# Seven graph hops and an attention block on one core: overflow sums held open at hop seams, bucket-pass work moved between ScalarE and VectorE, and a buffer of its own for hop 2's first matrices

## The chip, the core and the metric

One core of a Trainium2 chip runs the whole program. It has five engines that each take their instructions in order: PE (TensorE, matmuls), ACT (ScalarE), DVE (VectorE), POOL (GpSimd) and SP (SyncE, which here issues DMAs). The metric is the device time of one execution in microseconds (us), lower is better. Times of the profile are microseconds from the start of one profiled execution; "L844" is line 844 of the kernel before.

## The reference

A graph of 10,000 nodes and 160,000 directed edges, 128 features for each node. Seven times the features are propagated along the edges with a symmetric normalization. Each node then has eight tokens (its own features and the seven hops), which go through one self-attention block, and a readout weighs the eight results.

```python
h = x
toks = [x]
for _ in range(7):
    msg = h[src] * deg_inv_sqrt[src, None] * deg_inv_sqrt[dst, None]
    h = _segment_sum(msg, dst, N)
    toks.append(h)
tok = jnp.stack(toks, axis=1)                      # (N, K+1, D)
t = _layernorm(tok, axis=-1)
...
o = tok + jnp.einsum('nkd,de->nke', o, wo)
alpha = _softmax(jnp.einsum('nkd,d->nk', _layernorm(o, axis=-1), w_r), axis=-1)
return jnp.einsum('nk,nkd->nd', alpha, o)
```

## The kernel before, in words

**Layout.** The nodes are cut into 79 tiles of 128. The current features of all nodes lie in SBUF in a table `tab` (each value as a high and a low half of 16 bits, so a row has 256 columns), in two copies, one read and one written in a hop. A hop is done as matmuls with one-hot matrices: for one destination tile, 72 gather matmuls (L844) pick the source rows of its edges out of the table into PSUM tiles `p`, nine evictions (ACT L849 for five of them, DVE L851 for four) bring them to SBUF tiles `eb`, and 18 scatter matmuls (L819) add them into the destination's sum `acc` in PSUM. This is a *block*; a hop is 79 blocks, tiles 72 to 78 first and then 0 to 71. The blocks of a hop are numbered 0 to 78 in that order.

**Overflow rows.** An edge that doesn't fit into the fixed buckets of its tile is brought from a copy of the table in DRAM by an indirect DMA on POOL, `fetch` (L781). There are two of these for each tile: `og0` reads `tabh`, which holds the rows of the tiles from 72 on, and `og1` reads `tabd`, all rows; each is added with one more matmul (L804). The rows of the last tile of a hop reach `tabd` only after the hop's last block, so the `og1` of blocks 0 and 1 of the next hop (named `ogl`) come late: those two blocks add them at the close of the sum (L833), after their scatters. Closing a block also means a DVE reduction `s` (L835) and `entries` (L880 to L882: ACT, DVE, DVE), which make the next table's rows, and a scaling `r` on POOL (L889) and a store by SP. Scatters lag two evictions behind the gathers (`pend`), and the close of a block is done in the next one; between two hops stands a scaling step (a maximum over nodes, on PE, DVE and PE again: `pm`, `pb`).

**How hops are ordered.** Hops 2 to 7 are written block by block in Python and placed by the framework's scheduler; POOL, like the others, runs its queue in order. `ahead` asks the fetches of the block two further on; at the start of a hop it asks those of blocks 0 to 2 together.

**The second bucket pass and hop 1.** Before, a first pass over the edges has put them into buckets by source. The second pass places each bucket's edges by destination and makes the one-hot matrices `w` of each tile (written to DRAM as `gsd`, read again by the hops 2 to 7), and hop 1 runs beside it. It goes over 20 *quads* of four tiles (the first of three) in a software pipeline written by hand: the string FRONT is a list of words, each with a lag in sweeps, a letter for a step, and indices; `tc.manual_schedule` keeps this order on each engine. Sweep i does each word for quad i minus its lag. Steps that matter here: `O` (L493, one-hot of keys on DVE, L263), `X` (L517, a product `ux` on DVE for which `R` on PE waits, L524), `U` (L513, ACT), `a` (SP loads `rb` and `ra` from DRAM; one buffer for `rb`), `b` (L668, one DVE operation, 1408 columns of `w` from `rb`), `w` (L672, two ACT operations of 448 columns from `ra`), `G` (gather, L711), `x` (eviction, ACT L719 or DVE L721), `S` (scatter, L696 and L697) and `z` (DVE copies the in-degree, L735).

The eviction of the second pass picks its engine thus (before):

```python
if n < len(quads) - 1 or jj % 2 == 0:
    A.activation(e[:, :, 0:256], pv, AF.Copy, scale=8.0)
else:
    V.tensor_tensor(e[:, :, 0:256], pv, self.eight[:, :, None].to_broadcast([128, 2, 256]), op=ALU.mult)
```

The first matrices that hop 2 reads are loaded into a pool that is opened when the pools of hop 1 have been given back (L981). The attention's constants (L1100 to L1123) are made during hop 2; two of them start from iotas on POOL (L1106, L1116).

Of the kernel before, what the change touches and what calls it, by code (L numbers as in the profile page):

```python
# [7 lines left out]
F32 = mybir.dt.float32  # L8
# [16 lines left out]
CELL = 334  # L25
ROWS = 56
# [41 lines left out]
class Hops:  # L68
# [580 lines left out]
    def matrices(self, quads, Q):  # L649
# [17 lines left out]
        def b(q, g, t):  # L667
            V.tensor_scalar(q["w", g][:, NJ * 128:NJ * 128 + cut], q["rb", g], self.pid8, 0.125, op0=ALU.is_equal, op1=ALU.mult, saturate=False)  # L668
# [21 lines left out]
    def hop1(self, quads, Q):  # L690
# [23 lines left out]
        def x(q, g, t, n, jj):  # L714
            e = q["eb", g, jj] = ebuf[self.eb_i % len(ebuf)]
            self.eb_i += 1
            pv = q["p", g, jj].rearrange("p j h d -> p j (h d)")
            if n < len(quads) - 1 or jj % 2 == 0:
                A.activation(e[:, :, 0:256], pv, AF.Copy, scale=8.0)  # L719
            else:  # L720
                V.tensor_tensor(e[:, :, 0:256], pv, self.eight[:, :, None].to_broadcast([128, 2, 256]), op=ALU.mult)  # L721
# [50 lines left out]
    def fetch(self, t, i, src, name=None, after=None):  # L772
# [4 lines left out]
        else:  # L777
            o = self.ogp.tile([128, 256], F16, name=name or f"og{i}", bufs=2 if name else None)
# [6 lines left out]
    def block(self, t, w, tab, og, pend, lag, runs, first, evac, fin, lead=False, late=False, mid=None, ahead=None,  # L785
              after=None):


# [4 lines left out]
        def both(W, rows, start, stop=False):  # L793

            T.matmul(acc[0][:, :129], W, rows[:, 128:257], start=start, stop=False, skip_group_check=True)
            T.matmul(acc[0][:, :128], W, rows[:, :128], start=False, stop=stop, skip_group_check=True)


        def fetched(i, start=False, stop=False):
            W = w[:, (NG + i) * 128:(NG + i + 1) * 128] if i < NI else self.Sov[:, t, :]  # L800
            if first:
                both(W, og[i], False, stop)
                return
            T.matmul(acc[0][:, :256], W, og[i], start=start, stop=stop)  # L804

        def begin():
            acc.append(self.pacc.tile([128, 512], F32, name="acc", tag="acc"))
            for i in range(NI if late else NI + 1):
                fetched(i, start=i == 0)

        def scat(e, jj):
            if not acc:
                acc.append(self.pacc.tile([128, 512], F32, name="acc", tag="acc"))
            for j in range(e.shape[1]):
                J = 2 * jj + j
                if first:
                    both(w[:, J * 128:(J + 1) * 128], e[:, j], J == 0)
                else:
                    T.matmul(acc[0][:, :256], w[:, J * 128:(J + 1) * 128], e[:, j, :256], start=False, stop=J == NG - 1 and not late)  # L819
                if first and J == 0 and not lead:  # L820
                    for i in range(NI):
                        fetched(i)

        def close():
            if first:
                if lead:
                    for i in range(NI):
                        fetched(i)
                fetched(NI, stop=True)
                fin(t, acc[0][:, :128], acc[0])  # L830
                return
            if late:
                T.matmul(acc[0][:, :256], self.Sov[:, t, :], og[NI], start=False, stop=True)  # L833
            s = self.fp.tile([128, 128], F32, name="s")
            V.tensor_reduce(s, acc[0][:, 0:256].rearrange("p (h d) -> p d h", h=2), axis=X, op=ALU.add)  # L835
            fin(t, s, acc[0])
# [17 lines left out]
        jj = 0  # L854
        for i, n in enumerate(runs):
            for _ in range(n):
                gather(jj)
                if jj == 0 and not first and not mid:
                    ahead(self.ebuf[(self.eb_i - 1) % len(self.ebuf)][:, 0, 0:1])
                jj += 1  # L860
            if mid:
                mid(0)
            if not first:
                begin()
                if mid:
                    ahead()
            while len(pend) > lag:
                pend.pop(0)()
            if mid:
                mid(1)  # L870
            if after:
                after()
            if i == len(runs) - 1:
                pend.append(close)
            yield
# [17 lines left out]
    def run(self, ctx, att, nhop=K):  # L893
        tc, nc, V, A, T, G = self.tc, self.nc, self.nc.vector, self.nc.scalar, self.nc.tensor, self.nc.gpsimd
        with ExitStack() as c:
# [5 lines left out]
            G.memset(self.wB[:, 0], 0.0)  # L901
            base, self.ebuf = self.ebuf, []
            self.more_ebufs(self.bp, 8 - len(base))
            self.extra, self.ebuf = self.ebuf, base
            self.og1 = [[self.bp.tile([128, 260], F16, name=f"og{j}{b}") for b in range(2)] for j in range(NI + 1)]
            for o in (o for z in self.og1 for o in z):
                G.memset(o, 1.0)
            self.pass_a()
# [6 lines left out]
            Q = [dict() for _ in quads]  # L915
            words = [(int(z[0]), z[1], [int(k) for k in z[2:].split(".")]) for z in FRONT.split()]
            with tc.manual_schedule():
                do = {**self.place(quads, Q), **self.matrices(quads, Q), **self.hop1(quads, Q)}
                for i in range(len(quads) + max(z[0] for z in words)):
                    for late, z, more in words:  # L920
                        if 0 <= i - late < len(quads):
                            do[z](i - late, *more)
        with ExitStack() as c:
# [11 lines left out]
            pend = []  # L935
            for k in range(2, nhop + 1):
                i = 1 - k % 2
                tab, din = self.tab[i], (self.tabd[i], self.tabh[i])
# [20 lines left out]
                def fin(t, s, acc, k=k, ct=ct, last=last, i=i):  # L959
# [6 lines left out]
                order = [*range(4 * NG, NT), *range(4 * NG)]  # L966
# [605 lines left out]
```

## Time and profile before

| what | value |
|---|---|
| three timed executions, us | 3792.43, 3800.98, 3807.27 (median 3800.98) |
| the profiled execution's own time, us | 3793.14 |
| its span in the profile, us | 3791.4 |
| mean granted TensorE clock | 0.975 of full speed |
| first bucket pass | 0 to 345 us |
| second bucket pass and hop 1 | 345 to 1014.7 us |
| hops 2 to 7 | 1014.7 to about 3140 us |
| attention and readout | about 3146 us to the end |

How to read what follows. A row of a *timeline* has the start, the time from there to the end of the group, the engine, the line, the operation, output and input with their shapes, the number of instructions taken together, and in brackets the idle time just ahead of it with what ended it. "issue" is idle time in which the engine waited for nothing that the profile shows. A row of *waits* has the engine, the waiting tile and line, an arrow to what it waited for, then total us, number of times and longest. A row of *windows* has the stretch, its length, the busy time of PE, PE's weight loads, DVE, ACT and POOL with their instructions, the granted clock, the share of DMA and GB/s. A row of *groups* has line, engine, operation and shapes, the count, then busy us, mean ns of one, and idle time ahead with its releasers.

### The profile page before, as it was taken

The numbers are of one execution on the slowest core, as the hardware profiler recorded it, in microseconds if no ns is written. First come the engines' busy times: TensorE is split into PE (matmuls) and PEld (weight loads), VectorE is DVE, ScalarE is ACT, GpSimd is POOL, SyncE is SP. The second block draws the span as 40 slices with busy tenths as digits, with TensorE's granted clock in tenths as the row PEclk, the third lists the DMA queues.
The fourth block names the chain that finished last, engine by engine and source line by source line (L and its number), as shares of the span: only waits on it lengthen the run. The fifth ranks groups of instructions, "written<-read, shape, count | busy, mean of one in ns | idle before, by whom it ended". The sixth has DMA issues, their size and how long they took to land.

```text
span 3791.4 us, 174085 instructions
## 1 busy us (share of the span) xinstructions
PE 3563.0 (94%) x73922; PEld 2942.3 (78%) x73922; DVE 3030.7 (80%) x7077; ACT 2790.2 (74%) x7083; POOL 1687.0 (44%) x2231
## 2 busy tenths in 40 slices
PE   6777899999899999999999999999999998999997
PEld 4676677788688888887888788888878886777775
DVE  9999888899677777777777777777766665888888
ACT  7996688888766766766766676666656658888885
POOL 1000334444366656665666566566656661211111
PEclk8988899999999999999999999999999999999998
DMA  2011556566666666666666666666666552222220
GB/s 83 1 30 39 155 184 187 188 191 190 203 199 199 202 196 200 203 199 190 203 201 204 186 203 198 196 203 200 202 190 198 188 182 73 77 80 79 82 84 15
DMA packets 332729, 595.57 MB, mean 157 GB/s; under 512 B 57447, under 2 KB 225605, under 8 KB 326693
## 3 DMA queue, kind: packets, MB, share of 16 engines
q1 hardware_dynamic: 293989, 506.70, 42.9%
q0 software_dynamic: 35392, 72.55, 6.7%
q8 instruction: 579, 9.49, 1.0%
q10 hardware_dynamic: 2560, 5.12, 0.5%
q14 instruction: 209, 1.71, 0.2%
HBM read 455.49 MB, written 128.67 MB: 154 GB/s over the span
## 4 chain that ended last, share of the span: by engine, by line
PE 68%; DMA 2%; DVE 1%; issue 1%; ACT 1%; SPq 0%; ACTq 0%; DVEq 0%; POOLq 0%
PE p L844 26%; PE acc L819 24%; PE acc L804 4%; PE pv L1216 4%; PE pu L1200 4%; PE po L1235 2%; PE pt L1190 2%; PE ps L1265 1%; PE pf L1424 1%; PE sm L1271 1%; DMA og<-tabd,oidx 1%; DMA ogl<-tabd,oidx 0%; PE pf L1250 0%; DMA tabd<-tab 0%; ACT junk L1257 0%
## 5 line engine op out<-in xcount | busy, mean ns | idle before, releaser
L849 ACT ACTIVATE eb<-p 128x512 f16<-128x512 f32 x2370 | 1259.2, 601 | 506.7 <-PE p L844 296.3
L851 DVE TENSOR_TENSOR eb<-p,eight 128x512 f16<-128x512 f32 x1896 | 1220.3, 685 | 307.1 <-PE acc L819 187.0
L844 PE MATMUL p<-tab,w 128*32 128x256 f16 x34128 | 1036.0, 274 | 17.9 <-issue 12.3
L819 PE MATMUL acc<-eb,w 128*128 128x256 f16 x8532 | 1012.9, 273 | 2.3 <-DVE id L1119 1.6
L844 PEld LDWEIGHTS <-w 128*32 128x32 fp8e4 x34128 | 872.7, 97 | 155.2 <-issue 136.0
L819 PEld LDWEIGHTS <-w 128*128 128x128 fp8e4 x8532 | 835.8, 98 | 101.3 <-issue 3.2
L781 POOL DMA_INDIRECT og<-tabh,oidx x553 | 594.9, 1076 | 683.2 <-DVE eq L678 359.2
L781 POOL DMA_INDIRECT og<-tabd,oidx x541 | 577.4, 1067 | 559.0 <-PE acc L819 262.4
L719 ACT ACTIVATE eb<-p 128x512 f16<-128x512 f32 x695 | 373.8, 618 | 17.0 <-PE p L711 13.0
L889 POOL TENSOR_SCALAR r<-s,ctok 128x128 f32<-128x128 f32 x474 | 294.8, 622 | 47.3 <-DVE s L835 30.1
L880 ACT ACTIVATE tab<-s,c 128x128 f16<-128x128 f32 x395 | 158.5, 401 | 200.3 <-DVE eb L851 168.1
L881 DVE SCALAR_TENSOR_TENSOR tab<-s,c,tab 128x128 f16<-128x128 f32 x395 | 138.9, 352 | 180.6 <-issue 170.2
L1305 POOL TENSOR_TENSOR p<-e,in 128x1024 f32<-128x1024 f32 (+1 forms) x40 | 76.6, 1914 | 449.6 <-DVE e L1304 435.5
L1257 ACT ACTIVATE junk<-tab 128x128 f32<-128x128 f32 x626 | 248.4, 401 | 8.2 <-SPq L1541 6.8
L389 ACT ACTIVATE rs<-iof,rb 128x128 fp8e4<-128x128 f32 x832 | 251.6, 391 | 0.8
L711 PE MATMUL p<-tab,w 128*32 128x256 f16 x5688 | 205.7, 277 | 22.4 <-ACT eb L719 14.3
L835 DVE TENSOR_REDUCE s<-acc 128x128 f32<-128x256 f32 x474 | 196.4, 414 | 22.5 <-PE acc L833 14.5
L696 PE MATMUL acc<-eb,w 128*128 128x129 f16 x1422 | 204.2, 223 | 1.2 <-issue 0.8
L697 PE MATMUL acc<-eb,w 128*128 128x128 f16 x1422 | 202.3, 221 | 0.6 <-issue 0.6
L780 POOL COPY og<-eb 128x1 f16<-128x1 f16 x452 | 84.1, 186 | 252.2 <-ACT eb L849 252.1
L711 PEld LDWEIGHTS <-w 128*32 128x32 fp8e4 x5688 | 137.0, 96 | 58.2 <-issue 37.2
L1216 PEld LDWEIGHTS pv<-Wv,xT 128*64 128x64 f32 x2504 | 138.9, 137 | 44.8 <-ACT uT L1201 29.2
(322 smaller groups left out, 5233.9 us busy)
## 6 DMA issues: line engine op xcount, KB each, us to landing
w<-gsd SPq DMA_DIRECT2D x474, 592.0 KB
gsd<-w SPq DMA_DIRECT2D x79, 592.0 KB
tok<-r SPq DMA_DIRECT2D x546, 64.0 KB
tab<-tok SPq DMA_DIRECT2D x273, 128.0 KB
rb<-srow SPq DMA_DIRECT2D x79, 352.0 KB
tabd<-tab SPq DMA_DIRECT2D x396, 64.0 KB
ra<-srow SPq DMA_DIRECT2D x79, 224.0 KB
og<-tabh,oidx POOLq DMA_INDIRECT x553
```

The source lines that it names most:

```text
L389: A.activation(c["ro"][k][:, j - cuts[k][0], i, :], self.iof, AF.Abs_reciprocal_sqrt, scale=2.0 ** 21, bias=c["rb"][:, j - VP, i:i + 1], s ...
L696: T.matmul(acc[:, :129], W, rows[:, 128:257], start=start, stop=False, skip_group_check=True)
L711: T.matmul(p[32 * w:32 * w + 32, j], q["w", g][:, NJ * 128 + s * CAP:NJ * 128 + (s + 1) * CAP], tab[:, s, :], start=True, stop=True)
L719: A.activation(e[:, :, 0:256], pv, AF.Copy, scale=8.0)
L781: self.nc.gpsimd.indirect_dma_start(out=o[:, :256], out_offset=None, in_=src[0] if i == NI else src[1], in_offset=bass.IndirectOffsetOnAxi ...
L819: T.matmul(acc[0][:, :256], w[:, J * 128:(J + 1) * 128], e[:, j, :256], start=False, stop=J == NG - 1 and not late)
L844: T.matmul(p[32 * q:32 * q + 32, j], w[:, NJ * 128 + s * CAP:NJ * 128 + (s + 1) * CAP], tab[:, s, :], start=True, stop=True)
L849: A.activation(e[:, :n, 0:256], pv, AF.Copy, scale=8.0)
L851: V.tensor_tensor(e[:, :n, 0:256], pv, self.eight[:, :, None].to_broadcast([128, n, 256]), op=ALU.mult)
L889: self.nc.gpsimd.tensor_scalar(r, s, ct[:, t:t + 1], None, op0=ALU.mult)
L1216: T.matmul(p[64 * h:64 * h + 64, u - us[0], :], S[i]["xT"][:, h * m + q, 64 * c:64 * c + 64], Wv, start=True, stop=True, tile_position=(0, ...
L1257: A.activation(j, S[i]["x"][:, g, :], AF.Square, bias=S[i]["x"][:, g, 0:1], scale=-1.0, accum_out=R[i % 6][:, 0, g:g + 1])
```

## The change

It has seven parts.

1. `HEAD = 2`: for the first two quads (seven tiles) step `b` is done by two ACT operations of 704 columns instead of one DVE operation of 1408.
2. Evictions with odd number go to DVE in the last three quads instead of the last one.
3. The two first steps `O` are issued ahead of the first sweep.
4. The pool of the extra eviction tiles and of hop 1's overflow rows is opened after the first bucket pass.
5. Hop 2's first matrices have a buffer of their own, `wx`, loaded in the last sweep.
6. At the seams of hops the overflow sums are held open longer. Blocks 0 and 1 close after the scatters of blocks 2 and 3; blocks 2 and 3 sum into the other half of the PSUM tiles of blocks 0 and 1. Blocks 0 to 4 all add `og1` at their close. A table, LEAD, says in which block and behind which eviction each fetch of the first blocks is asked, and the first four `og0` of the next hop are asked in blocks 77 and 78. `og0` has six buffers instead of three.
7. The attention's two iotas are made when its object is made, at the program's start.

```diff
+HEAD = 2
...
         def b(q, g, t):
+            if q["n"] < HEAD:
+                new(q, g)
+                for a in range(0, cut, cut // 2):
+                    A.activation(q["w", g][:, NJ * 128 + a:NJ * 128 + a + cut // 2], q["rb", g][:, a:a + cut // 2], AF.Abs_reciprocal_sqrt,
+                                 scale=2.0 ** 14, bias=self.off, saturate=False)
+                return
             V.tensor_scalar(q["w", g][:, NJ * 128:NJ * 128 + cut], q["rb", g], self.pid8, 0.125, op0=ALU.is_equal, op1=ALU.mult, saturate=False)
...
-            if n < len(quads) - 1 or jj % 2 == 0:
+            if n < len(quads) - 3 or jj % 2 == 0:
...
+                early = [("O", 0, 0), ("O", 0, 1)]
+                for z, *a in early:
+                    do[z](*a)
+                sweeps = len(quads) + max(z[0] for z in words)
+                for i in range(sweeps):
+                    if i == sweeps - 1:
+                        nc.sync.dma_start(ready[0], self.GSd[quads[0][0]])
...
+            LEAD = {0: ((0, 4, 0), (0, 5, 0), (None, 0, 1)), 1: (), 2: ((0, 1, 1), (6, 2, 1)), 3: ((0, 3, 1), (6, 4, 1)),
+                    4: ((0, 5, 1), (6, 6, 0)), 5: ((0, 6, 1), (6, 7, 0)), 6: ((0, 7, 1), (0, 8, 0), (6, 8, 1))}
+            for m in range(4):
+                ask(2, m, 0)
...
+                    if n in (1, 2):
+                        held.append(pend.pop())
+
+                    def open_acc(n=n):
+                        if n in (2, 3):
+                            return half[n - 2][:, 256:512], False
+                        z = self.pacc.tile([128, 512], F32, name="acc", tag="acc")
+                        if n < 2:
+                            half[n:] = [z]
+                        return z[:, 0:256], True
...
+                    self.block(t, w, tab, og[k][n], pend, 2, lambda jj: jj in (0, 2, 4, 5, 7), fin, n < 5,
+                               (lambda part, n=n: scale(part, n)) if n < 2 and not last else None, ahead,
+                               held.pop(0) if n in (2, 3) else None, open_acc)
...
+        self.pr, self.ci = (cp.tile([128, w], I32, name=name) for name, w in (("apr", 1), ("aci", 128)))
+        self.nc.gpsimd.iota(self.pr, pattern=[[0, 1]], base=0, channel_multiplier=1)
+        self.nc.gpsimd.iota(self.ci, pattern=[[1, 128]], base=0, channel_multiplier=0)
```

An entry of LEAD reads (behind which eviction, or None for behind none; which block's; `og0` or `og1`). Three places of the queues follow. A name ends in a number that tells tiles apart.

PE before, at the seam of hops 3 and 4, end of block 1: its scatters (into `acc_44724`), the late matmul that closes block 0 (`acc_44589`, with block 0's fetched rows `ogl_44593`), and the first gather of block 2.

```order
L819 LDWEIGHTS w_44620
L819 MATMUL acc_44724<-eb6_24294,w_44620 128x256
L833 LDWEIGHTS Sov_252
L833 MATMUL acc_44589<-ogl_44593,Sov_252 128x256
L844 LDWEIGHTS w_44759
L844 MATMUL p_44761<-tab1_65,w_44759 32x256
```

PE after, the matmul that closes block 0 (now L811, with `ogl_44549`), behind the scatters of block 2 (L807, into the same PSUM tile `acc_44631`, other half) and ahead of the first gather of block 3 (L822).

```order
L807 MATMUL acc_44631<-eb0_258,w_44778 128x256
L807 LDWEIGHTS w_44778
L807 MATMUL acc_44631<-eb1_260,w_44778 128x256
L811 LDWEIGHTS Sov_256
L811 MATMUL acc_44631<-ogl_44549,Sov_256 128x256
L822 LDWEIGHTS w_44906
L822 MATMUL p_44908<-tab1_65,w_44906 32x256
```

The matmul that needs block 0's late rows has moved from the end of block 1 to the end of block 2.

POOL before, the same seam: the rows fetched for blocks 0 to 2 (`tabd1` and `tabh1` are the DRAM copies that hop 4 reads), and the two scalings `r` around them.

```order
L889 TENSOR_SCALAR r_44489<-s_44483,ctok0_248 128x128
L781 DMA og0_44726<-tabh1_169,oidx_253 128x256
L781 DMA ogl_44593<-tabd1_167,oidx_253 128x256
L781 DMA ogl_44595<-tabd1_167,oidx_253 128x256
L781 DMA og1_44597<-tabd1_167,oidx_253 128x256
L781 DMA og1_44728<-tabd1_167,oidx_253 128x256
L781 DMA og1_44774<-tabd1_167,oidx_253 128x256
L889 TENSOR_SCALAR r_44756<-s_44749,ctok1_24269 128x128
```

POOL after, the same place. A COPY (L787) writes one column of the buffer from an eviction tile, so that the fetch behind it starts after that eviction.

```order
L858 TENSOR_SCALAR r_44527<-s_44521,ctok0_252 128x128
L787 COPY og0_44543<-eb5_24313 128x1
L787 COPY og0_44546<-eb5_24313 128x1
L788 DMA og0_44543<-tabh1_173,oidx_257 128x256
L788 DMA og0_44546<-tabh1_173,oidx_257 128x256
L788 DMA ogl_44549<-tabd1_171,oidx_257 128x256
L787 COPY ogl_44790<-eb9_24317 128x1
L788 DMA ogl_44790<-tabd1_171,oidx_257 128x256
L787 COPY og1_44853<-eb1_260 128x1
L788 DMA og1_44853<-tabd1_171,oidx_257 128x256
L858 TENSOR_SCALAR r_44903<-s_44896,ctok1_24289 128x128
```

Five fetches from `tabd1` that stood in a row are now one behind two `og0`, and then one at a time behind an eviction each.

DVE before, in the second pass, between the products `ux` of the last two quads (the second of them is at 945.93 us of the trace): the last two words of one placing step, then the next ones.

```order
L599 TENSOR_SCALAR sh_22193<-sh_22193 128x4
L600 TENSOR_SCALAR oidx_253<-sh_22193,cell0_5561 128x4
L604 TENSOR_SCALAR fl_22227<-ov_21354 128x32
L607 TENSOR_REDUCE ct_22229<-fl_22227 128x4
L678 TENSOR_TENSOR eq_22268<-dsl0_5542,io8_5552 128x640
```

DVE after, the same place.

```order
L600 TENSOR_SCALAR sh_22211<-sh_22211 128x4
L601 TENSOR_SCALAR oidx_257<-sh_22211,cell0_5555 128x4
L728 TENSOR_TENSOR eb1_5617<-p_22168,eight_226 128x2x256
L728 TENSOR_TENSOR eb0_258<-p_22187,eight_226 128x2x256
L728 TENSOR_TENSOR eb1_260<-p_22200,eight_226 128x2x256
L605 TENSOR_SCALAR fl_22245<-ov_21372 128x32
```

Three evictions of the second pass now stand in DVE's queue here; with three more at other places, six stand between the two products.

More of the change, by code (lines that the diff above doesn't have):

```diff
@@ L783, in fetch, with block @@
         return o
-    def block(self, t, w, tab, og, pend, lag, runs, first, evac, fin, lead=False, late=False, mid=None, ahead=None,
-              after=None):
+    def block(self, t, w, tab, og, pend, lag, evac, fin, late, mid, ahead, after, open_acc):
         nc, V, A, T, G = self.nc, self.nc.vector, self.nc.scalar, self.nc.tensor, self.nc.gpsimd
         acc = []
[L793 to L804, printed above, removed]
@@ L806, in begin @@
         def begin():
-            acc.append(self.pacc.tile([128, 512], F32, name="acc", tag="acc"))
+            m, start = open_acc()
+            acc.append(m)
             for i in range(NI if late else NI + 1):
-                fetched(i, start=i == 0)
+                W = w[:, (NG + i) * 128:(NG + i + 1) * 128] if i < NI else self.Sov[:, t, :]
+                T.matmul(m, W, og[i], start=start and i == 0, stop=False, skip_group_check=True)
         def scat(e, jj):
-            if not acc:
-                acc.append(self.pacc.tile([128, 512], F32, name="acc", tag="acc"))
@@ L814, in scat @@
             for j in range(e.shape[1]):
                 J = 2 * jj + j
[L816 to L822, printed above, removed]
-        def close():
[L825 to L831, printed above, removed]
+                T.matmul(acc[0], w[:, J * 128:(J + 1) * 128], e[:, j, :256], start=False, stop=J == NG - 1 and not late, skip_group_check=True)
@@ L852, in gather @@
             pend.append(lambda: scat(e[:, :n], jj))
[L854 to L875, printed above, removed]
+        for jj in range(NG // 2):
+            gather(jj)
+            ahead(jj, self.ebuf[(self.eb_i - 1) % len(self.ebuf)][:, 0, 0:1])
+        if mid:
+            mid(0)
+        begin()
+        while len(pend) > lag:
+            pend.pop(0)()
+        if mid:
+            mid(1)
+        if after:
+            after()
+        pend.append(close)
     def entries(self, t, s, i):
@@ L918, in run @@
                 do = {**self.place(quads, Q), **self.matrices(quads, Q), **self.hop1(quads, Q)}
-                for i in range(len(quads) + max(z[0] for z in words)):
+                early = [("O", 0, 0), ("O", 0, 1)]
[5 more added lines that the diff above has]
+                        nc.sync.dma_start(ready[0], self.GSd[quads[0][0]])
                     for late, z, more in words:
-                        if 0 <= i - late < len(quads):
+                        if 0 <= i - late < len(quads) and (z, i - late, *more) not in early:
                             do[z](i - late, *more)
```

65 lines of the change are left out of this document (33 added, 32 removed).

## The prediction

> **What bounds the kernel now.** I read the busy shares first, then the chain that ended last, then what PE waits for, then PE's share by stage. PE first:
>
> ```profile
> PE 3563.0 (94%) x73922; PEld 2942.3 (78%) x73922; DVE 3030.7 (80%) x7077; ACT 2790.2 (74%) x7083; POOL 1687.0 (44%) x2231
> PE 68%; DMA 2%; DVE 1%; issue 1%; ACT 1%; SPq 0%; ACTq 0%; DVEq 0%; POOLq 0%
> PE p L711 <- ACT eb L719: 14.3, 13, 2.8
> PE p L844 <- issue: 12.3, 30, 1.1
> PE acc L833 <- DMA ogl<-tabd,oidx: 7.6, 4, 3.8
> 1040.00:1390.00 350.00, 345.95 (x7248) 292.23 (x7247) 273.07 (x567) 239.23 (x471) 216.27 (x310) 1.00 0.65 199
> ```
>
> PE is busy 94% of the span and is the chain. Inside a hop (last row: PE, PEld, DVE, ACT and POOL busy, then the clock) it works 345.95 of 350 us, so no edit can gain in a hop's middle, where its order is unchanged. What can be had are PE's waits: in hops 2 to 7 the fetches for the late overflow matmul (7.6 us) and "issue" (12.3 us), in the second pass the evictions (14.3 us). To see where hops lose time I take the first gather of the last block of a hop (block 78) and of block 4 of the next, for the five seams between hops 2 and 7:
>
> ```profile
> 1371.15 2.15 PE L844 MATMUL p<-tab,w 128*32 128x256 f16 x72
> 1398.27 2.15 PE L844 MATMUL p<-tab,w 128*32 128x256 f16 x72
> 1722.55 2.15 PE L844 MATMUL p<-tab,w 128*32 128x256 f16 x72
> 1752.34 2.17 PE L844 MATMUL p<-tab,w 128*32 128x256 f16 x72
> 2076.75 2.15 PE L844 MATMUL p<-tab,w 128*32 128x256 f16 x72
> 2105.29 1.75 PE L844 MATMUL p<-tab,w 128*32 128x256 f16 x52
> 2430.80 2.15 PE L844 MATMUL p<-tab,w 128*32 128x256 f16 x72
> 2457.32 2.20 PE L844 MATMUL p<-tab,w 128*32 128x256 f16 x72
> 2781.80 2.15 PE L844 MATMUL p<-tab,w 128*32 128x256 f16 x72
> 2809.90 2.32 PE L844 MATMUL p<-tab,w 128*32 128x256 f16 x72
> ```
>
> From 1398.27 to 1722.55 are 74 blocks: 4.38 us each. Five blocks should take 21.91. The seams took 27.12, 29.79, 28.54, 26.52 and 28.10: they lose 5.2, 7.9, 6.6, 4.6 and 6.2 us, **30.5 in all**. How they lose it, on the costliest (PE, then POOL's first and last of five fetches, the clock over 11 us) and on the first (PE, POOL, the clock):
>
> ```profile
> 1733.86 0.35 PE L161 MATMUL pb<-r,ones 1*128 1x1 f32 x2 [0.19 <-DVE r L174]
> 1736.81 0.27 PE L833 MATMUL acc<-ogl,Sov 128*128 128x256 f16 x1 [0.42 <-DMA ogl<-tabd,oidx]
> 1739.50 0.33 PE L844 MATMUL p<-tab,w 128*32 128x256 f16 x3 [1.05 <-issue]
> 1733.87 0.95 POOL L781 DMA_INDIRECT ogl<-tabd,oidx  x1 [2.67 <-DMA tabd<-tab]
> 1738.87 0.95 POOL L781 DMA_INDIRECT og<-tabd,oidx  x1 [0.30 <-issue]
> 1737.00:1748.00 11.00, 8.24 (x98) 5.27 (x101) 4.45 (x10) 3.35 (x7) 5.55 (x8) 0.69 0.45 130
> 1387.63 0.27 PE L833 MATMUL acc<-ogl,Sov 128*128 128x256 f16 x1 [2.65 <-DMA ogl<-tabd,oidx]
> 1382.66 0.95 POOL L781 DMA_INDIRECT ogl<-tabd,oidx  x1 [2.87 <-DMA tok<-r]
> 1374.00:1388.00 14.00, 11.16 (x209) 9.04 (x210) 8.85 (x28) 6.01 (x13) 7.16 (x9) 1.00 0.60 174
> ```
>
> A late fetch holds block 0's closing (0.42 to 2.65 us here); while POOL sends five fetches back to back, 1.25 us apart (1733.87 to 1738.87), PE stops on "issue", once for 1.05 us; and the clock drops to 0.69, some 3.4 us more (31% of 11).
>
> **Hop seams, hops 2 to 7.** Blocks 0 and 1 now close after the scatters of blocks 2 and 3, one block later, and POOL sends at most three fetches together. With T0 the start of block 0's gather, block 0 closes at about T0+13.1 (three blocks). Its fetch, still third at POOL behind the last row write, is there by T0+9 to +12: before, its matmul began 1387.63 - 1382.66 = 5.0 us after the issue at the latest. The wait goes in all five seams. Next late are the fetches of blocks 1 (needed T0+17.5) and 2 (T0+15.8); block 2's is asked behind its own eviction 6 and by the same spacing lands at T0+14.3 to +16.3, so up to 0.5 us may stay. Two closes also fall to DVE in block 3, about 0.2 us over a block. From nothing lost (-30.5) I take off 0.75 a seam for the scale step between two hops, which stays (pb's 0.35 and its wait of 0.19, and as much as the wait once more), and 0.5 for the items above: 30.5 - 6.3 = 24.2. **Taken: -24**; ends -28 and -8 (only the closings' 7.6 us goes).
>
> **Seam of hops 1 and 2.** PE's last matmul of hop 1 with the first gathers of blocks 0 and 2, the clock between, SP's first load of matrices, and two rows of DVE:
>
> ```profile
> 1014.48 0.22 PE L697 MATMUL acc<-og,Sov 128*128 128x128 f16 x1
> 1018.86 4.03 PE L844 MATMUL p<-tab,w 128*32 128x256 f16 x72 [4.16 <-DMA tabd<-tab]
> 1035.22 1.05 PE L844 MATMUL p<-tab,w 128*32 128x256 f16 x30
> 1016.00:1023.00 7.00, 4.14 (x74) 3.14 (x75) 2.95 (x11) 1.79 (x3) 4.12 (x6) 0.58 0.92 315
> 1014.83 0.32 SPq L981 DMA_DIRECT2D w<-gsd  x1
> 1015.93 0.16 DVE L735 COPY indeg<-acc 128x1 f32<-128x1 f32 x1 [0.88 <-ACT r L744]
> 1020.21 0.23 DVE L1104 TENSOR_SCALAR cen<-ident 128x128 f32<-128x128 f32 x1 [2.68 <-DMA tok<-r]
> ```
>
> The releaser named for 4.16 us is a row write that nothing here reads; what had to land was the load issued at 1014.83 (about 4 us). From 1014.70 to 1035.22 two blocks took 20.5 us instead of 8.8: 11.8 lost. The own buffer is loaded a sweep earlier, so the gather can begin when DVE's last copy of in-degrees has ended, at about 1016.1. What is late next: POOL's first overflow fetch still goes at the end of hop 1, and `cen` waits for the token write that landed at 1020.2 with evictions queued behind it on DVE; PE's four banks p then fill and it stops for up to 2.8 us. Iotas no longer stand behind eight fetches. 1016.1 + 8.8 + 2.8 + 0.8 for the scale step gives block 2 at 1028.5 instead of 1035.2. **Taken: -6.5**; -9 if `cen` costs nothing, -3 if the clock is again near half while block 0 runs (it was 0.58). An idle time of 2.65 us left it at 1.00 (window from 1374), 4.16 did not; the new idle of 1.4 is on the good side. The Trainium skill, "TensorE: Matmul & The Clock Gate", Part 1, gives about 3.4 us of idleness as what halves the clock; those two rows agree, but the fall to 0.69 behind idles of about 1 us does not. By the page alone this term would be the same.
>
> **Head of the second pass.** Seven one-hot halves (b) go from DVE to two ACT activations each. Groups and a window of that stretch, and two waits:
>
> ```profile
> L668 DVE TENSOR_SCALAR w<-rb,pid 128x1408 fp8e4<-128x1408 int16 x79 | 74.7, 945 | 8.7 <-DMA rb<-srow 8.7
> L672 ACT ACTIVATE w<-ra,off 128x448 fp8e4<-128x448 int16 x158 | 108.6, 688 | 48.9 <-DMA ra<-srow 48.9
> 385.00:425.00 40.00, 32.94 (x650) 26.77 (x649) 34.57 (x69) 21.84 (x52) 11.42 (x7) 0.82 0.50 151
> 414.62 0.67 ACT L672 ACTIVATE w<-ra,off 128x448 fp8e4<-128x448 int16 x1 [3.08 <-DMA ra<-srow]
> 419.92 0.16 DVE L735 COPY indeg<-acc 128x1 f32<-128x1 f32 x1 [3.76 <-ACT r L744]
> ```
>
> DVE sheds 7 x 0.945 = 6.6 us where it is 86% busy and ACT 55%. ACT has no 704-column row: a pair costs between 2 x 0.688 = 1.38 and that by columns, 2.16; I take 1.65, near the 448 row, 11.6 in all. Little of the relief reaches PE: DVE already idles 3.76 us at 419.92 waiting for ACT, so only the first three b (2.8 us) stand in front of busy DVE. Against that ACT, 3.08 us late at 414.62 by a transfer, gets 1.65 more in front of four evictions that PE's next gathers need, twice in the head, and the single buffer of rb comes free 0.7 later. **Taken: +1**; -3 (relief alone) to +4 (two b and rb).
>
> **Tail of the second pass.** Thirty-two more evictions of quads 17 and 18 go from ACT to DVE:
>
> ```profile
> L721 DVE TENSOR_TENSOR eb<-p,eight 128x512 f16<-128x512 f32 x16 | 10.5, 686 | 6.9 <-PE p L711 5.3 <-PE acc L697 1.5
> 950.00:975.00 25.00, 20.57 (x502) 16.20 (x502) 16.52 (x50) 23.84 (x57) 7.52 (x7) 1.00 0.63 196
> 945.93 2.13 DVE L517 TENSOR_TENSOR ux<-oh,U 128x3800 f16<-128x3800 f16 x1
> ```
>
> They add 32 x 0.686 = 22 us to DVE, idle 8.5 of these 25 us, and relieve ACT, busy 23.8 of them. That is PE's gain: PE is idle for 4.4, and I give the quad after it a third of that, 6 at best. But six of the 32 come in DVE's order ahead of `ux` at 945.93, with no idle time before it: up to 6 x 0.686 = 4.1 us, and the last quad's placing waits for that product. **Taken: +0.5**; -6 to +4.
>
> The other edits are costed at nothing: the memsets and the two iotas run on POOL while it is idle early, and the two first one-hots fall in a DVE wait whose successor waits for PE anyway; uncovered, either is under 2.5 us.
>
> **Rivals.** (a) "Issue" stays: the stalls belong to the code at a hop's start and not to the fetches sent together. For it: DVE and ACT idle with PE there. Against: the middles show almost none. Then only the closings' 7.6 us goes: -7.6 - 6.5 + 1.5 = -12.6. The Trainium skill, "Runtime: NRT & Kernel Launch", Instruction fetch mechanics, says that code is fetched ahead in sequence and mostly hidden; by it neither the code nor the fetches would cause these stops, and (a) would hold; the stop of 1.05 us speaks for something that hides badly under load. (b) All at its best, -28 - 9 - 3 - 4 = -44. (c) The rebalanced ends become the bound, all 22 us of evictions behind a busy DVE less the 6 that ACT frees: +16 instead of +0.5, sum -14. (d) The other side: the late closings, now five a seam instead of two, each come 1 us late because POOL asks one block at a time behind an eviction, and repeated stops hold the clock down over five blocks: 5 + 0.75 + 3.4 x 21.9/11 = 12.5 a seam, 62.5 in all instead of 30.5: +32 - 6.5 + 1.5 = +27. It decides above 7.1 us a seam ((30.5 + 6.5 - 1.5)/5). For it: stops of 1 us took the clock to 0.69 once. Against: only one of five fetches has no slack.
>
> **How the numbers follow.** The sum is -24 - 6.5 + 1 + 0.5 = -29. Against the profiled execution's own 3793.1 us (span 3791.4) that is 3764. It lies 7.8 under the median of the three runs, 3801.0; all four times average 3798.2, 5 above it, so I forecast **3769**. Chances: forecast 0.50 (own range 3756 to 3781), (a) 0.24 at 3786, (b) 0.10 at 3754, (c) 0.10 at 3784, (d) 0.06 at 3825. The range 3745 to 3793 leaves out (d) and a little at both ends. Half a per cent, what a measurement can tell from no change, is 19 us: faster beyond it takes nearly all of the forecast and (b) and a little of (a), 0.62; within it most of (a) and (c), 0.31; slower 0.07.
>
> **What would show it.** In the trace after: block 78 to block 4 takes 22.5 to 23.5 us at each seam; no wait of the late closing above 0.5 us; "issue" before the gathers under 4 us in all instead of 12.3; hop 2's first gather within 1.5 us of hop 1's last matmul and at full clock; second pass as long as before within 3 us; attention unchanged. Gathers still stopping on "issue" with no five fetches beside them would make (a) right and this wrong.

## The result, and the profile after

The changed kernel takes 3834.4 us (median of 6 runs, 3830.2 to 3836.3) against 3800.6 of before: the ratio is **1.0095** (95% interval 1.0081 to 1.0110). It is slower by 34 us by the medians and by 36 by the ratio, above the whole range of the prediction. The profiled execution has a span of 3833.4 us, 42.0 more than before's.

The busy shares and PE's waits of the kernel after:

```profile
PE 3585.5 (94%) x73922; PEld 2937.0 (77%) x73922; DVE 3030.7 (79%) x7102; ACT 2747.3 (72%) x7065; POOL 1690.1 (44%) x2287
PE p L822 <- issue: 24.7, 53, 1.5
PE p L822 <- DVE eb L829: 3.3, 12, 0.3
PE acc L811 <- DMA og<-tabd,oidx: 1.6, 2, 0.9
```

The late closings wait 1.6 us instead of 7.6: what the change aims at came true. But "issue" ahead of the gathers has doubled, 24.7 us instead of 12.3. Idle time tells only a part: PE's busy time grew by 22.5 us (from 3563.0) for the same 73922 instructions. A gather matmul counts as busy for 0.27 us while the next one starts 0.027 us behind it, so a short stop between two of them hides in the busy time. To see where the time goes, the span is cut at the first gather of blocks 0, 5, 9 and 77 of each hop; the sums, in us, are taken from those starts in the two traces:

```
stretch                                       before    after    more
to the last scatter of hop 1                  1014.5   1019.7    +5.2
from there to block 5 of hop 2                  34.2     35.4    +1.2
blocks 0 to 5, hops 3 to 7                     139.5    119.9   -19.6
blocks 5 to 9, hops 2 to 7                     106.1    129.0   +22.9
blocks 9 to 77, hops 2 to 7                   1791.2   1815.2   +24.0
block 77 to the next hop's block 0, 5 times     45.9     51.7    +5.8
block 77 of hop 7 to the end                   660.1    662.5    +2.4
```

(The first row is not firm: the end of hop 1 moves by up to 6 us among profiles with the same order of this pass, 1019.4 to 1025.6 with the new ends of it, 1008.0 and 1013.9 in e10 and e9 below.) The first five blocks of a hop gain, and more than twice as much is lost next to them and in the middles. The middles had been left out of the forecast because their order is unchanged. One of them, hop 4 from block 9 to block 77, before and after:

```profile
1774.20 2.15 PE L844 MATMUL p<-tab,w 128*32 128x256 f16 x72
2072.38 2.15 PE L844 MATMUL p<-tab,w 128*32 128x256 f16 x72
```

```profile
1793.97 2.15 PE L822 MATMUL p<-tab,w 128*32 128x256 f16 x72
2096.70 2.17 PE L822 MATMUL p<-tab,w 128*32 128x256 f16 x72
```

298.2 us have become 302.7. All of it lies between gathers of one block: from each gather's start to the next one's the trace has 133.3 us instead of 128.7, and for the scatters 126.2 in both. Of the 68 blocks 19 are longer than 4.45 us (2 before), 17 of these by 0.1 to 0.3 us. Two groups of instructions, over the whole program, show what moved: POOL's `og0` fetches and DVE's reduction `s`, before and then after.

```profile
L781 POOL DMA_INDIRECT og<-tabh,oidx x553 | 594.9, 1076 | 683.2 <-DVE eq L678 359.2 <-PE acc L697 131.4 <-POOL og L780 122.0
L835 DVE TENSOR_REDUCE s<-acc 128x128 f32<-128x256 f32 x474 | 196.4, 414 | 22.5 <-PE acc L833 14.5 <-PE p L844 3.5 <-PE acc L819 3.0
```

```profile
L788 POOL DMA_INDIRECT og<-tabh,oidx x553 | 587.9, 1063 | 424.9 <-POOL og L787 206.7 <-PE acc L704 134.1 <-DVE eq L685 33.2
L813 DVE TENSOR_REDUCE s<-acc 128x128 f32<-128x256 f32 x474 | 199.3, 420 | 87.8 <-PE acc L807 69.7 <-PE acc L811 4.2 <-issue 2.8
```

A fetch now stands 206.7 us in all behind the COPY ahead of it, not 122.0, and `s` waits 69.7 us for the scatters that end the sum, not 3.0. One middle block at the same place of hop 3, POOL before, then POOL and DVE after:

```profile
1482.61 0.19 POOL L780 COPY og<-eb 128x1 f16<-128x1 f16 x1 [0.57 <-ACT eb L849]
1483.07 1.02 POOL L781 DMA_INDIRECT og<-tabh,oidx  x1 [0.27 <-POOL og L780]
```

```profile
1484.29 0.18 POOL L787 COPY og<-eb 128x1 f16<-128x1 f16 x1 [0.48 <-ACT eb L827]
1484.99 1.02 POOL L788 DMA_INDIRECT og<-tabh,oidx  x1 [0.51 <-POOL og L787]
1486.32 0.94 POOL L788 DMA_INDIRECT og<-tabd,oidx  x1 [0.30 <-issue]
```

```profile
1487.01 0.42 DVE L813 TENSOR_REDUCE s<-acc 128x128 f32<-128x256 f32 x1 [0.49 <-PE acc L807]
```

The COPY is followed by its fetch after 0.27 us before and 0.51 after. The queues say why: the wait for an older fetch of POOL (DMASW) stood at the COPY and now stands at the fetch (before, then after):

```
L780 COPY og_46937<-eb_24296 128x1 [waits DMASW7_49,Activation_49]
L781 DMA og_46937<-tabh_169,oidx 128x256 [waits Pool_49]

L787 COPY og_47862<-eb_260 128x1 [waits Activation_49]
L788 DMA og_47862<-tabh_173,oidx 128x256 [waits DMASW3_49,Pool_49]
```

The fetches use eight semaphores in turn, and a fetch waits for the one that used its semaphore last, eight fetches back. With three buffers the COPY writes a buffer whose last fetch, six fetches back, must be waited for, which covers the other wait too. With six buffers that fetch is so old that the COPY has to wait for none, and the fetch keeps its own wait, behind the COPY. The traces agree: in the six middles 402 wait instructions for a fetch's landing have the COPY's line before, and none after. In the blocks at 1478.68 and 1483.05 after, the landing waited for was over 12 us old, so the 0.24 us is the price of the wait's place and not of a late transfer.

Why a quarter of a microsecond matters is in the times at which PE's completion signals were recorded, here from the first gather of a block (before at 1481.44, after at 1478.68, and after at 1782.52, block 7 of hop 4). A bar stands where signals are missing that should have come:

```
         POOL issues indirect fetches     PE's signals arrive
before   1.63-2.66, 3.37-4.33             0.43 0.65 0.87 1.08 1.30 1.52 1.74 | 2.95 3.04 3.07 3.11 3.17
after    1.95-2.97, 3.28-4.24             0.51 0.65 0.87 1.09 1.30 1.52 1.74 1.96 2.53 2.57 | 3.98
after    0.23-1.21, 1.53-2.49, 4.45-5.47  | 3.24 3.34 3.43 3.52 3.61 3.83 4.40 | 5.78 5.81 5.85 5.90
```

PE signals every 0.22 us as gathers end. **While POOL issues an indirect fetch, signals that fall due arrive late, in a bunch, up to about 1.3 us behind one fetch and nearly 3 us behind two in a row.** Over hops 2 to 7 of before (1060 to 3100 us) 1712 signals of PE fell due 0.2 to 1.2 us after the start of an `og0` fetch, and 15 of them were recorded within 0.1 us; of the 416 due in the next 0.2 us it was 405. ACT and DVE can't evict without them, PE runs out of PSUM tiles, and the profile calls PE's wait "issue". In the first row the gap covers a place where no stop follows; in the second it covers the signal that ends the sum (the last one, due at about 2.9), so `s`, the next table's rows and the next evictions are late and a later gather stops for 0.2 to 0.3 us; in the third it covers a gather from its start. That third block on PE and POOL:

```profile
1783.49 0.38 PE L822 MATMUL p<-tab,w 128*32 128x256 f16 x5 [0.25 <-issue]
1784.24 0.31 PE L822 MATMUL p<-tab,w 128*32 128x256 f16 x4 [0.36 <-issue]
1784.97 0.38 PE L822 MATMUL p<-tab,w 128*32 128x256 f16 x5 [0.42 <-issue]
1785.71 0.63 PE L822 MATMUL p<-tab,w 128*32 128x256 f16 x14 [0.36 <-issue]
```

```profile
1780.00 1.02 POOL L788 DMA_INDIRECT og<-tabd,oidx  x1 [0.39 <-POOL og L787]
1781.32 0.95 POOL L788 DMA_INDIRECT og<-tabh,oidx  x1 [0.30 <-issue]
1782.75 0.98 POOL L788 DMA_INDIRECT og<-tabd,oidx  x1 [0.27 <-issue]
1784.05 0.95 POOL L788 DMA_INDIRECT og<-tabd,oidx  x1 [0.32 <-issue]
```

LEAD asks three fetches in block 6 and the ordinary order adds one: four in five microseconds, and block 7 takes 7.1 us instead of 4.4.

### The profile page after: what moved, and what is told of

It is laid out like the page before. It is cut to its first block, busy times and chain, and to the rows that moved or that the text cites. A ratio compares the mean times of both kernels' runs of the same rounds, so it can differ in the third digit from the quotient of the medians.

```text
span 3833.4 us, 174189 instructions
## 1 busy us (share of the span) xinstructions
PE 3585.5 (94%) x73922; PEld 2937.0 (77%) x73922; DVE 3030.7 (79%) x7102; ACT 2747.3 (72%) x7065; POOL 1690.1 (44%) x2287
## 5 line engine op out<-in xcount | busy, mean ns | idle before, releaser
L827 ACT ACTIVATE eb<-p 128x512 f16<-128x512 f32 x2370 | 1218.4, 606 | 414.0 <-PE p L822 375.9
L829 DVE TENSOR_TENSOR eb<-p,eight 128x512 f16<-128x512 f32 x1896 | 1198.4, 684 | 293.2 <-PE p L822 160.0
L822 PE MATMUL p<-tab,w 128*32 128x256 f16 x34056 | 1054.0, 273 | 28.5 <-issue 18.5
L807 PE MATMUL acc<-eb,w 128*128 128x256 f16 x8514 | 1010.7, 273 | 0.2 <-issue 0.2
L822 PEld LDWEIGHTS <-w 128*32 128x32 fp8e4 x34056 | 868.6, 96 | 180.9 <-issue 156.0
L807 PEld LDWEIGHTS <-w 128*128 128x128 fp8e4 x8514 | 833.9, 98 | 97.4 <-issue 0.4
L788 POOL DMA_INDIRECT og<-tabh,oidx x553 | 587.9, 1063 | 424.9 <-POOL og L787 206.7
L726 ACT ACTIVATE eb<-p 128x512 f16<-128x512 f32 x663 | 358.6, 617 | 23.0 <-PE p L718 16.6
L813 DVE TENSOR_REDUCE s<-acc 128x128 f32<-128x256 f32 x474 | 199.3, 420 | 87.8 <-PE acc L807 69.7
L718 PE MATMUL p<-tab,w 128*32 128x256 f16 x5688 | 206.2, 277 | 23.1 <-ACT eb L726 14.6
L787 POOL COPY og<-eb 128x1 f16<-128x1 f16 x502 | 93.1, 187 | 244.7 <-ACT eb L827 241.2
```

The costliest lines, as they stand in the source:

```text
L718: T.matmul(p[32 * w:32 * w + 32, j], q["w", g][:, NJ * 128 + s * CAP:NJ * 128 + (s + 1) * CAP], tab[:, s, :], start=True, stop=True)
L788: self.nc.gpsimd.indirect_dma_start(out=o[:, :256], out_offset=None, in_=src[0] if i == NI else src[1], in_offset=bass.IndirectOffsetOnAxi ...
L807: T.matmul(acc[0], w[:, J * 128:(J + 1) * 128], e[:, j, :256], start=False, stop=J == NG - 1 and not late, skip_group_check=True)
L822: T.matmul(p[32 * q:32 * q + 32, j], w[:, NJ * 128 + s * CAP:NJ * 128 + (s + 1) * CAP], tab[:, s, :], start=True, stop=True)
L827: A.activation(e[:, :n, 0:256], pv, AF.Copy, scale=8.0)
L829: V.tensor_tensor(e[:, :n, 0:256], pv, self.eight[:, :, None].to_broadcast([128, n, 256]), op=ALU.mult)
```

## The experiments

Theory S is the one above. Against it stood M (the middles are slower through something else of the change), I (the "issue" stalls belong to the code of a hop's first blocks), Q (POOL being busy is what counts), and for the second pass H (the head), T (the tail) and N (what they cost is made up again).

**Six buffers alone, in the kernel before.**

```diff
-name=name or f"og{i}", bufs=2 if name else None)
+name=name or f"og{i}", bufs=2 if name else 3 + 3 * (i < NI))
```

> The kernel before with one edit: og0 has six buffers instead of three. Theory S (while POOL issues an indirect fetch, PE's completion signals reach ACT and DVE late, by up to 1.3 us; with six buffers the wait for the fetch's own DMA slot stands behind the COPY instead of ahead of it, so each middle fetch goes 0.25 us later and its withheld signals fall on another part of the block): the stretch from block 9 to block 77 grows from 298.1 us to 300.5 to 304 in each hop, the whole by 15 to 30 us over before. Rival M (the middles became slower through something else of the change): 298.1 in each hop, the whole within 5 us of before.

3851.9 us, ratio 1.0142 (1.0107 to 1.0176): slower than the whole change, and by 53 us instead of 15 to 30. The six middles take 1811.8 us instead of 1791.2, 301.2 to 303.6 each; S holds there and M falls. Not one wait instruction of the middles has the COPY's line. Not expected: another 22 us between block 77 and the next block 0 (68.2 instead of 45.9), where free buffers let POOL send the next hop's fetches early and in a row, five fetches 1.25 to 1.33 us apart.

**Three buffers again in the middles of the changed kernel.**

```diff
-bufs=2 if name else 3 + 3 * (i < NI))
+bufs={"ogl": 2, "ogs": 6}.get(name, 3))
...
-"ogl" if j == NI and m < 2 else None, after)
+("ogl" if m < 2 else None) if j == NI else "ogs" if m < 9 else None, after)
```

> The changed kernel, but og0 of blocks 0 to 8 of each hop has a ring of six buffers of its own and og0 of all later blocks the three buffers of before. Theory S: blocks 9 to 77 take 298.2 us again (within 0.7) in each hop instead of 300.6 to 304.2, the whole is 20 to 27 us below the changed kernel, near 3810; blocks 5 to 9 stay at 20 to 24 us. Rival M: the middles stay above 300.5 and the whole within 5 us of 3834.

3815.8 us, 1.0044 (1.0026 to 1.0062), 18.6 below the changed kernel, a little less than the 20 to 27 expected. The middles take 1790.6 us, before's own, and the 402 wait instructions stand at the COPY again. The same row of DVE's `s` and hop 4's middle:

```profile
L813 DVE TENSOR_REDUCE s<-acc 128x128 f32<-128x256 f32 x474 | 197.0, 416 | 12.6 <-PE acc L811 5.7 <-PE p L822 2.7 <-PEq L1538 1.4
```

```profile
1790.96 2.15 PE L822 MATMUL p<-tab,w 128*32 128x256 f16 x72
2089.31 2.15 PE L822 MATMUL p<-tab,w 128*32 128x256 f16 x72
```

`s` no longer waits for the scatters. Both directions of one edit are thus shown to set the middles.

**No more than two fetches in a block.** As e2, eight `ogs` buffers, and

```diff
+LEAD = {0: ((0, 4, 0), (0, 5, 0)), 1: ((0, 6, 0), (0, 7, 0), (None, 0, 1)), 2: ((0, 1, 1), (6, 2, 1)), 3: ((0, 3, 1), (6, 4, 1)),
+        4: ((0, 5, 1), (6, 8, 0)), 5: ((0, 6, 1), (6, 7, 1)), 6: ((0, 8, 1),)}
```

> As the run before it, and the table of the first blocks' fetches rewritten so that no block asks more than two from block 2 on (block 6 asked three) and block 1 asks og0 of blocks 6 and 7. Theory S: blocks 5 to 9 go from 20 to 24 us to 17.5 to 19 in hops 3 to 7, the whole is another 10 to 20 us lower, 3790 to 3800. Rival I (the issue stalls belong to the code of a hop's first blocks, whatever POOL does): blocks 5 to 9 stay at 20 to 24 and the whole within 4 us of the run before.

3802.4 us, 1.0013 (0.9997 to 1.0028), 13.4 below e2. Blocks 5 to 9 fell from 130.3 (e2) to 110.2 us in all, so I falls. But blocks 0 to 5 of hops 3 to 7 grew from 119.6 to 131.4, which I hadn't expected: POOL runs its queue in order, so the two `og0` asked in block 1 waited behind block 0's late rows and made a new row of four:

```profile
1746.57 0.95 POOL L788 DMA_INDIRECT ogl<-tabd,oidx  x1 [3.72 <-issue]
1747.52 0.35 POOL L787 COPY ogs<-eb 128x1 f16<-128x1 f16 x2
1748.01 0.98 POOL L788 DMA_INDIRECT ogs<-tabh,oidx  x1
1749.30 0.95 POOL L788 DMA_INDIRECT ogs<-tabh,oidx  x1 [0.30 <-issue]
1750.26 0.19 POOL L787 COPY ogl<-eb 128x1 f16<-128x1 f16 x1
1750.73 0.98 POOL L788 DMA_INDIRECT ogl<-tabd,oidx  x1 [0.27 <-issue]
```

**What one more operation of POOL costs.** The kernel before, with an extra in every second block from 20 to 58, into a tile `spare`:

```diff
+if jj != (5 if k == 4 else 8):
+    return
+o = self.ogp.tile([128, 256], F16, name="spare", bufs=3)
+G.tensor_copy(o[:, 0:1], e)
+if k in (3, 4):
+    G.indirect_dma_start(out=o[:, :256], out_offset=None, in_=din[1], in_offset=...)
+elif k == 5:
+    G.dma_start(out=o[:, :256], in_=self.tabd[0][0:128, :256])
+else:
+    G.tensor_copy(o[:, :256], self.Sov[:, 0:2, :].rearrange("p a d -> p (a d)"))
```

> The kernel before with one extra POOL operation in every second block from 20 to 58 (20 in a hop), into a spare tile that nothing reads: in hop 3 an indirect fetch behind eviction 8, which falls into the next gather; in hop 4 an indirect fetch behind eviction 5, which falls into the scatters; in hop 5 a plain DMA of the same 64 KB issued by POOL behind eviction 8; in hop 6 an elementwise copy on POOL of about 1 us behind eviction 8. Theory S: hop 3 grows by 0.8 to 2.7 us for each extra (16 to 54 us), hop 4 by less than half of that, hop 6 by under 0.1 each; the plain DMA tells whether it is POOL's issuing as such or the indirect form. Rival Q (POOL being busy is what counts, since r and the fetches come later): hops 3 and 6 grow alike. Rival I: none grows by more than 3 us.

This kernel has one execution, 3861.1 us. From block 9 to 77 hops 3 to 6 took 325.1, 322.7, 302.0 and 300.3 us, and 298.1 without: 27.0, 24.6, 3.9 and 2.2 us for 20 extras. **An extra indirect fetch costs 1.35 us, the same bytes as a plain DMA of POOL 0.2, a POOL copy 0.1.** POOL was busy for 0.97 us in an extra fetch, 0.58 in the plain DMA and only 0.40 in the copy, which was meant to last 1 us. But signals of PE that fell due while the copy ran were all recorded within 0.1 us (31 of 31), with the plain DMA 49 of 54, with the scaling `r` of 0.62 us 523 of 538, and with an extra fetch or up to 0.25 us behind it 3 of 78. So Q and I fall. The indirect fetch "in the scatters" was to be cheap and cost 1.23: it pushed the ordinary fetch behind it into the next gather. One of hop 3's, POOL and then PE:

```profile
1506.68 0.98 POOL L982 DMA_INDIRECT spare<-tabh,oidx  x1 [0.27 <-issue]
1508.72 1.02 POOL L781 DMA_INDIRECT og<-tabh,oidx  x1 [0.27 <-POOL og L780]
```

```profile
1506.08 1.53 PE L844 MATMUL p<-tab,w 128*32 128x256 f16 x43
1508.04 0.60 PE L844 MATMUL p<-tab,w 128*32 128x256 f16 x13 [0.43 <-issue]
1508.90 0.62 PE L844 MATMUL p<-tab,w 128*32 128x256 f16 x16 [0.26 <-issue]
```

**Every seam fetch alone, and the two ends.** As e2, but all fetches of blocks 0 to 6 and of the next hop are asked behind evictions 0 and 6:

```diff
+LEAD = {0: ((0, 4, 0), (6, 5, 0)), 1: ((0, 6, 0), (6, 0, 1)), 2: ((0, 1, 1), (6, 2, 1)), 3: ((0, 3, 1), (6, 4, 1)),
+        4: ((0, 5, 1), (6, 7, 0)), 5: ((0, 6, 1), (6, 8, 0)), 6: ((0, 7, 1), (6, 8, 1))}
...
-elif jj == 0 and not last:
-    m = 2 * (n + 2 - NT)
-    ask(k + 1, m, 0, e)
-    ask(k + 1, m + 1, 0)
+elif jj in (0, 6) and not last:
+    ask(k + 1, 2 * (n + 2 - NT) + jj // 6, 0, e)
```

> The changed kernel with the middles' three og0 buffers (as e2), and every fetch of a hop's first seven blocks and last two asked singly: at most two a block, one behind eviction 0 and one behind eviction 6. Theory S: block 77 to the next hop's block 0 takes 9.2 to 9.6 us instead of 10.35, blocks 0 to 5 take 22.5 to 24.5 and blocks 5 to 9 17.5 to 18.5 in hops 3 to 7, hop 2's start stays slow (30 to 34); the whole 15 to 25 us under e3, 3778 to 3788. Rival I (the stalls belong to a hop's first blocks): not over 5 us under e3.

3793.1 us, 0.9979 (0.9966 to 0.9992): faster than before and 9 us under e3, so I falls again, though the forecast was 3778 to 3788. Blocks 0 to 5 are back at 120.7 us; blocks 5 to 9 stay at 117.7, because the fetch for block 9 is asked on top of block 6's two. Three more went with it: `HEAD = 0` (e6), `len(quads) - 1` in the evictions (e7), and both (e8).

> As e5, but step b of the first two quads is on DVE again (HEAD = 0). The second pass and hop 1 ended at 1014.5 and 1017.2 us in two profiles of the old ends, at 1019.7, 1025.6 and 1025.1 in three of the new ones. Theory H (ACT's b ahead of evictions is the loss): hop 1 ends at 1018 or earlier and the whole is 3 to 8 us under e5. Rival T (the evictions moved to DVE in the tail are): within 2 us of e5.

> As e5, but only the last quad's odd evictions are on DVE, as before. Theory T: hop 1 ends at 1018 or earlier and the whole is 3 to 8 us under e5. Theory H: within 2 us of e5.

> As e5, with both ends of the second pass as before. Both theories: hop 1 ends at 1014 to 1018, the whole 5 to 9 us under e5 and 20 to 30 us under before, near 3772. If neither end matters: as e5.

3794.2, 3793.5 and 3787.9 us (0.9989, 0.9983, 0.9968 with 0.9954 to 0.9981). Neither end alone moves the whole by more than its runs scatter, so H and T both fail as stated; both together take 5 us off. e8 is 12 us below before, not the 20 to 30 expected. The ends were then tried each alone in the kernel before:

> The kernel before with step b of the first two quads on ACT, and nothing else. By the start of the eighth product ux, the profiles with b on DVE stood at 440.0 to 442.7 us, those with b on ACT at 443.5 to 445.3. Theory H: the eighth ux starts at 443.5 to 445.5 and the whole is 2 to 6 us slower than before. Rival N (the head's loss is made up later in the pass): the same eighth ux, and the whole within 2 us of before.

> The kernel before with the odd evictions of the last three quads on DVE instead of the last one's, and nothing else. In profiles with them on DVE the last two products ux stand 17.7 us apart, and 119.4 to 120.2 us lie between the start of the 37th ux and the end of hop 1, against 14.1 and 114.3 to 119.1. Theory T: 17.7 us, 119 to 121 us, and the whole 2 to 5 us slower than before. Rival N (what DVE loses ACT's relief gives back): 17.7 us but 116 or less, and the whole within 2 us of before.

3798.1 and 3800.3 us against 3796.1 of the same runs of before: 1.0007 (0.9995 to 1.0018) and 1.0009 (0.9997 to 1.0021). Both intervals hold no change as well, so neither cost is shown. The tail's local cost is there. The last two `ux` of the pass, before and in e12:

```profile
931.84 2.13 DVE L517 TENSOR_TENSOR ux<-oh,U 128x3800 f16<-128x3800 f16 x1
945.93 2.13 DVE L517 TENSOR_TENSOR ux<-oh,U 128x3800 f16<-128x3800 f16 x1
```

```profile
929.29 2.13 DVE L517 TENSOR_TENSOR ux<-oh,U 128x3800 f16<-128x3800 f16 x1
947.19 2.13 DVE L517 TENSOR_TENSOR ux<-oh,U 128x3800 f16<-128x3800 f16 x1
```

14.1 us have become 17.9. With ACT's b the eighth `ux` began at 444.0 (e11) instead of 442.7, but profiles with DVE's b range from 440.0 to 443.6 (e4), so the head's local cost isn't clear. That each end costs a few us of the whole isn't proven: e6 and e7, which take one of them back, gained nothing. Hop 1's end varies by up to 6 us among profiles of the same order, so it isn't used to decide.

**Hop 2's start.** As e8; hop 2's first four `og0` get tiles of their own, fetched in the last four sweeps (e9):

```diff
+if i >= sweeps - 4:
+    m = i - sweeps + 4
+    G.indirect_dma_start(out=first[m][:, :256], out_offset=None, in_=self.tabh[1],
+                         in_offset=bass.IndirectOffsetOnAxis(ap=self.oidx[:, 4 * NG + m, 0:1], axis=0))
```

> As e8, but the first four overflow fetches of hop 2 have buffers of their own and are issued one in each of the last four sweeps of the second pass, so POOL doesn't issue seven in a row while hop 2's first block gathers (1020.5 to 1029.2 us in the changed kernel, where that gather took 10 us instead of 2.1). Theory S: hop 2's block 0 to 5 goes from 31.3 to 24 to 27 us, the whole 4 to 7 us under e8, near 3782. Rival C (hop 2's start is slow for the clock, or for hop 1's last writes): 30 us or more, as e8.

3786.7 us, 0.9969 (0.9953 to 0.9986). The part in question did as S says: hop 2's blocks 0 to 5 take 26.3 us (e8 31.3), so C falls. The whole doesn't show those 5 us: its ratio to before is that of e8 (0.9968) within the noise. The first gather of hop 2 after, of which the first and one of the stops are shown, and in e9:

```profile
1021.38 1.49 PE L822 MATMUL p<-tab,wx 128*32 128x256 f16 x48 [1.49 <-issue]
1026.15 0.45 PE L822 MATMUL p<-tab,wx 128*32 128x256 f16 x3 [1.07 <-issue]
```

```profile
1015.50 2.23 PE L822 MATMUL p<-tab,wx 128*32 128x256 f16 x72 [1.34 <-DVE indeg L742]
```

**The ordinary pace from block 7 on.** As e9, but the next hop's `og0` are asked from block 76 on, one block earlier, so that the table ends in step (e10). `ogs` has eight buffers here, and hop 2's fifth `og0` is asked at that hop's start:

```diff
+LEAD = {0: ((0, 5, 0), (6, 6, 0)), 1: ((0, 7, 0), (6, 0, 1)), 2: ((0, 1, 1), (6, 2, 1)), 3: ((0, 3, 1), (6, 4, 1)),
+        4: ((0, 5, 1), (6, 8, 0)), 5: ((0, 6, 1), (6, 7, 1)), 6: ((0, 8, 1),)}
+if not last and (n + 2 >= NT and jj in (0, 6) or n + 3 == NT and jj == 6):
+    ask(k + 1, 2 * (n + 3 - NT) - 1 + jj // 6, 0, e)
```

> As e9, and the next hop's og0 are asked from block 76 on, so that the ordinary order of fetches starts again at block 7 without three in a row (in e5 the fetch for block 9 fell into block 7's gather, 5.8 us instead of 4.37). Theory S: blocks 5 to 9 take 17.5 to 18.2 instead of 19.2 to 20.6, the whole 6 to 10 us under e9, near 3775. Rival I: as e9 within 3 us.

**3781.6 us, 0.9953 (0.9937 to 0.9970)**: below before and after. Blocks 5 to 9 take 109.9 us (e9 117.8, before 106.1, after 129.0), 17.9 to 19.0 each, so I falls there. The whole is 5 us under e9, a little less than expected, and that step is not clear of the noise of the two by itself. PE's largest waits in its hops:

```profile
PE p L822 <- issue: 6.0, 20, 0.4
PE acc L811 <- DMA og<-tabd,oidx: 2.2, 3, 1.1
```

## Why the prediction was wrong, point by point

- *"No edit can gain in a hop's middle, where its order is unchanged"*, and so nothing was put down for a loss there. This is the step that failed first. The order did stay, but a wait moved within it, and six middles lost 24.0 us. The six buffers were put at nothing without a reason; which instruction of the pair COPY and fetch would carry the wait was never asked. With this one edit alone in the kernel before, the middles lose 20.6 us (e1), and with it taken back in the changed kernel they lose nothing (e2).
- **Hop seams, -24 us.** The wait for late rows did go. By the forecast's own measure, block 78 to block 4, the five seams took 126.1 us instead of 140.1: -14.0, inside the ends given. Inside it block 78 lost 5.8; blocks 77 and 78 now each ask two `og0` of the next hop together. And the seam doesn't end at block 4: other fetches moved out of it fell on blocks 5 to 9 (+22.9). "POOL sends at most three fetches together" was wrong on the change's own table, by which four go within five microseconds in blocks 6 and 7 and seven in a row at hop 2's start, and three were taken as harmless; measured, an extra fetch costs 1.35 us. The drop of the clock at the seams did go: from block 78 to block 4 it was 1.00 at all five after, and 0.89, 0.94 and 0.94 at three of them before.
- **Seam of hops 1 and 2, -6.5 us.** Block 2 began 20.5 us behind hop 1's last matmul, as before. PE idled only 1.49 us, as forecast, but POOL's seven fetches from 1020.5 to 1029.2, of which the prediction named the first as late and priced none, stretched block 0's gather to 9.7 us. Without them there (e9) hop 1's end to block 5 takes 27.9 us instead of 34.2: the term's size came out near the forecast, but the change lacked what it needed.
- **The clock.** In e9 an idle time of 1.34 us kept it: the gather of 72 takes 2.23 us, and the granted clock from 1015.50 to 1025 is 1.00. This agrees with the Trainium skill, "TensorE: Matmul & The Clock Gate", Part 1, by which about 3.4 us of idleness halve it. The forecast's full clock failed in the changed kernel all the same: it was 0.72 from 1021.38 to 1031, behind an idle time of 1.49 us and with no stop above 1.1 us. Repeated short stops lower the clock too, as the 0.69 of the prediction's rows had shown.
- **Head, +1, and tail, +0.5.** ACT's b came out as costed (14 of 704 columns, 11.6 us in all), and the last `ux` is 3.7 to 3.8 us late, near the 4.1 that I set against ACT's relief. What these cost of the whole is not shown for either alone; together it is 5 us by the medians of e5 and e8, more than the 1.5 of the forecast.
- **Rivals.** (a) had the stalls stay, which they did, but for another reason: not a hop's code but POOL's fetches hold PE. The sign named for it, stops with no five fetches beside them, could not tell the two apart. The prediction's aside that well hidden code would let (a) hold is the wrong way round, since (a) needs the code to stall PE. (d) gave the right side by a wrong mechanism: the closings weren't late, 1.6 us of waits against the 25 that it needed, and the seams got faster.
- **Signs.** Hop 2's early first gather came, but not its full clock. Block 78 to block 4 took 24.9 to 25.5 us instead of 22.5 to 23.5, a late closing waited 0.9, and "issue" took 24.7 instead of under 4.
- **A slip.** The four times average 3798.5, not 3798.2, which changes nothing in the forecast.

## What to carry to other kernels

When buffers are added to a ring, look at which instruction now carries the wait for an old transfer: a wait that was covered ahead of a pair can reappear between its two halves and shift everything behind it. Indirect fetches on POOL have to be spread, not only counted: with two a block in their usual places `s` waited 12.6 us in all (e2), and a third cost 1.2 to 1.35 us at both places where it was tried. "Issue" idle time on PE with ACT and DVE idle at the same moment is worth a look at what POOL is issuing just then, before code loading is blamed.

## What the runs showed of the hardware

Completion signals of PE were recorded up to 1.3 us late while POOL issued one indirect DMA of 128 rows (0.95 to 1.02 us of POOL's time), though PE's gathers don't read what it fetches; a plain DMA from POOL of the same size (0.58 us) cost 0.2 us of the kernel's time and a POOL copy (0.40 us) 0.1. It isn't PE's signals alone: of the 1352 signals of ACT and DVE that fell due 0.4 to 1.2 us after the start of an `og0` fetch in hops 2 to 7 of before, 134 were recorded on time. Many of theirs have no record at all (of ACT's 2675 in these hops 1505 have one, of DVE's 3118 1985, of PE's 5487 5445), so how late they come the traces don't tell.

The Trainium skill, "SBUF — State Buffer", SBUF: two separate sides, describes a lock that POOL and DVE share and says that PE and ACT never wait in it; the runs neither need nor exclude that lock for DVE, but here PE's signals, which ACT waits for as well, come late. Where signals are held was not tried and stays open; that the records of all three engines show it speaks against a place in PE, unless for ACT and DVE only the record is lost.
